# Engine orders by list scheduling, folding by column blocks and held weight loads in a linear-attention and gated-FFN kernel

## The chip, the cores and the metric

One core of a Trainium2 chip. The metric is device time in microseconds (us) of the whole program, on real inputs, with results compared with the reference. A bank is one of eight pieces, of 512 columns each, of the memory that matmuls write (PSUM); the programs here let results in the same bank take turns. The granted clock is the share of TensorE's full clock that the profile shows as let through. Engines: PE (TensorE matmul), PEld (its weight loads), DVE (VectorE), ACT (ScalarE), POOL (GpSimd), SP (which issues DMAs).

## The reference

```python
xn = layernorm(x)                                    # x: 2048 tokens x 512
out = x + A(xn) + B(xn)

# A: linear attention, 32 heads of 16
q, k, v = split(xn @ wqkv)
pq, pk  = q @ w_phi, k @ w_phi                       # per head
phi(p)  = concat(softmax(p), softmax(-p))            # for pq and pk
kv = phi_k^T v ; z = sum(phi_k) ; o = (phi_q kv) / (phi_q z + 1e-6)
A  = o @ wo
# B: gated FFN, 512 -> 1376 -> 512
B  = (gelu(xn @ w_gate) * (xn @ w_up)) @ w_down
```

Both kernels multiply `w_phi` into the Q and K weights first ("folding"), so that one projection gives `pq` or `pk`. The softmax denominators of K are row sums of exponentials; they are put on the values (value scaling), so that the sum over tokens (value accumulation, `kv_acc`) is a plain matmul chain.

## The kernel before

Tokens come in 16 tiles of 128. A tile is normalised on DVE, transposed (the first four on PE, the other twelve by DMA), projected to Q, K and V on PE, and exponentiated on ACT. POOL makes the row sums of the K exponentials in four steps, and the reciprocal standard deviation of the normalisation (`rstd`); DVE scales the values; PE accumulates them. The FFN follows in four chunks of 512 tokens, with 11 column blocks each; values that are not done by then, attention and output go beside it. The program is written in one sequence, and each engine runs its part in exactly that sequence. Waits are derived from buffers read and written. A unit, in the code, is one K or Q projection with what is written beside it; K and Q take two banks in turn. The parts that matter (cut):

```python
def op(self, ename, fn, reads=(), writes=(), extra=()):
    E = self.engs[ename]
    waits = self._resolve(E, self._deps_of(reads, writes, extra))
    ...
    E.ops.append((waits, fn, (E.sem, 1)))        # order on an engine = order of writing
...
proj_k(3, 1)
for t in range(8, 12):
    ln_stats(t)                                  # DVE, ahead of values 1 and 2
ln_rstd(8, 4)
v_recip(1); v_scale(1, 2)
v_recip(2); v_scale(2, 3)
...
units = []                                       # K and Q alternate
for s in range(3):
    for m in range(4):
        units.append(("k", 4 + 4 * s + m)); units.append(("q", s, m))
for m in range(4):
    units.append(("q", 3, m))
for u, un in enumerate(units):
    b = u % 2
    if u in (1, 2, 3, 4):      ln_norm(7 + u); xt_dma(7 + u)       # tiles 8 to 11
    ...
    if u in (10, 11, 12, 13):  ln_norm(2 + u); xt_dma(2 + u)       # tiles 12 to 15
    ... # proj_k or proj_q of the unit
    if u < 3:                  kv_acc(u)
    if u % 4 == 3:             proj_v(nv, 4); v_recip(nv); v_scale(nv, 4); nv += 1
    if u % 4 == 1 and u > 4:   kv_acc(nv - 1)
    if u % 3 == 2 and nbig < 5:
        big_loads(nbig); nbig += 1               # gate, up, wo, down: issued on POOL
```

wq is transposed by DMA; wk by PE, with two copies of 128x1024. Each fold makes a row block of the folded weights and needs all transposed columns.

The softmax here doesn't subtract the row's maximum and nothing guards it: scores larger than these inputs give would overflow.

Of the kernel before, what the change touches and what calls it, by code (L numbers as in the profile page):

```python
# [6 lines left out]
ALU = mybir.AluOpType  # L7
ACTF = mybir.ActivationFunctionType

P = 128  # L10
# [14 lines left out]
class _Handle:  # L25
    __slots__ = ("key", "val", "sem", "clock")

    def __init__(self, key, val, sem, clock):
        self.key = key
        self.val = val  # L30
        self.sem = sem
        self.clock = clock


class Buf:

    def __init__(self, name, aliases=()):
        self.name = name
        self.last_write = None
        self.readers = []  # L40
        self.aliases = list(aliases)


class _Eng:
    def __init__(self, name, sem):
        self.name = name
        self.sem = sem
        self.ops = []
        self.count = 0
        self.known = {}  # L50


class _DmaSlot:
    def __init__(self, sid, sem):
        self.sid = sid
        self.sem = sem
        self.count = 0
        self.last = None


class Sched:
    def __init__(self, eng_sems, dma_sems):
        self.engs = {n: _Eng(n, s) for n, s in eng_sems.items()}
        self.pools = {}
        k = 0
        for qn, sems in dma_sems.items():
            slots = []
            for s in sems:
                slots.append(_DmaSlot(k, s))
                k += 1  # L70
            self.pools[qn] = [slots, 0]

    def _resolve(self, E, deps):
        need = {}
        for h in deps:
            if h is None:
                continue
            if E.known.get(h.key, 0) >= h.val:
                continue
            cur = need.get(h.key)  # L80
            if cur is None or cur.val < h.val:
                need[h.key] = h
        waits = []
        for key in sorted(need.keys(), key=lambda x: str(x)):
            h = need[key]
            if E.known.get(key, 0) >= h.val:
                continue
            waits.append((h.sem, h.val))
            if E.known.get(key, 0) < h.val:
                E.known[key] = h.val  # L90
            for k2, v2 in h.clock.items():
                if E.known.get(k2, 0) < v2:
                    E.known[k2] = v2
        return waits

    @staticmethod
    def _deps_of(reads, writes, extra):
        deps = list(extra)
        for b in reads:
            deps.append(b.last_write)  # L100
            for a in b.aliases:
                deps.append(a.last_write)
        for b in writes:
            deps.append(b.last_write)
            deps.extend(b.readers)
            for a in b.aliases:
                deps.append(a.last_write)
                deps.extend(a.readers)
        return deps

    @staticmethod
    def _update(h, reads, writes):
        for b in reads:
            b.readers.append(h)
        for b in writes:
            b.last_write = h
            b.readers = []

    def op(self, ename, fn, reads=(), writes=(), extra=()):
        E = self.engs[ename]  # L120
        waits = self._resolve(E, self._deps_of(reads, writes, extra))
        E.count += 1
        idx = E.count
        clock = dict(E.known)
        clock[E.name] = idx
        h = _Handle(E.name, idx, E.sem, clock)
        E.ops.append((waits, fn, (E.sem, 1)))
        self._update(h, reads, writes)
        return h

    def dma(self, qname, fn, reads=(), writes=(), extra=()):
        E = self.engs[qname]
        slots, nxt = self.pools[qname]
        slot = slots[nxt % len(slots)]
        self.pools[qname][1] = nxt + 1
        deps = self._deps_of(reads, writes, extra)
        if slot.last is not None:
            deps.append(slot.last)
        waits = self._resolve(E, deps)
        slot.count += 1  # L140
        val = 16 * slot.count
        key = ("d", slot.sid)
        clock = dict(E.known)
        clock[key] = val
        h = _Handle(key, val, slot.sem, clock)
        E.ops.append((waits, fn, (slot.sem, 16)))
        slot.last = h
        self._update(h, reads, writes)
        return h

    def all_slots(self):
        res = []
        for qn, (slots, _) in self.pools.items():
            res.extend(slots)
        return res


def _replay(eng, E):
    for waits, fn, inc in E.ops:
        for sem, val in waits:  # L160
            eng.wait_ge(sem, val)
        ins = fn(eng)
        if inc is not None:
            ins.then_inc(inc[0], inc[1])


def bass_parallel_sum__linear_kernel_hedgehog__glu_gated_geglu__prompt_kernel(
# [14 lines left out]
    with ExitStack() as es, nc.allow_low_precision("bf16 softmax factors"):  # L182
# [34 lines left out]
        wk_nat = hT[:, 1, 0:4, :]  # L217
        wkT = hT[:, 1, 4:8, :]
        wqT = hT[:, 0, 0:4, :]

# [4 lines left out]
        NVS = 3  # L225
# [28 lines left out]
        def bank16(b):  # L254
# [6 lines left out]
             "act": [sem(f"dq_act{i}") for i in range(4)],  # L261
             "pool": [sem(f"dq_pool{i}") for i in range(6)]},
        )
        op = S.op
        dma = S.dma

        def bufs(name, n):
            return [Buf(f"{name}{i}") for i in range(n)]

# [6 lines left out]
        B_hT = bufs("hT", 2)  # L276
        B_wknat = Buf("wknat", aliases=[B_hT[1]])
        B_wkT = [Buf(f"wkT{i}", aliases=[B_hT[1]]) for i in range(2)]
        B_wqT = Buf("wqT", aliases=[B_hT[0]])
        B_hT[1].aliases = [B_wknat] + B_wkT  # L280
        B_hT[0].aliases = [B_wqT]
# [3 lines left out]
        B_Ek = bufs("Ek", NT)  # L285
        B_st = bufs("st", 3)
        B_S = bufs("S", NT)
        B_vs = bufs("vs", NVS)
        B_Eq = bufs("Eq", NST * 8)
        B_kvr = Buf("kvr")  # L290
        B_kvrm = Buf("kvrm")
        B_r, B_t, B_den, B_rden, B_cf, B_o = (bufs(n, NB) for n in ("r", "t", "den", "rden", "cf", "o"))
# [4 lines left out]
        B_ob = bufs("ob", 4)  # L297


        def load_x(t, extra=()):  # L300
            dma("sp", lambda e, t=t: e.dma_start(x_all[:, t, :], x2[t * P:(t + 1) * P, :]), writes=[B_x[t]], extra=extra)

        dma("act", lambda e: e.dma_start(
            wphi[:], A_w_phi.rearrange("(j hl) d f -> (hl d) j f", j=4)), writes=[B_wphi])
        load_x(0)
        dma("act", lambda e: e.dma_start(
            wk_nat, A_wqkv[:, 512:1024].rearrange("(i p) c -> p i c", p=P)), writes=[B_wknat])
        load_x(1)
        dma("act", lambda e: e.dma_start(
            wv_sb[:], A_wqkv[:, 1024:1536].rearrange("(i p) c -> p i c", p=P)), writes=[B_wv])  # L310
        load_x(2)
        load_x(3)
        load_x(4, extra=[B_wknat.last_write])
        for t in range(5, 8):
            load_x(t)
        dma("sp", lambda e: e.dma_start_transpose(wqT, A_wqkv[:, 0:512]), writes=[B_wqT])
        for t in range(8, NT):
            load_x(t)


        op("dve", lambda e: e.memset(warm[:], 0.0), writes=[B_warm])
        op("pool", lambda e: e.memset(ones_f[:], 1.0), writes=[B_ones])
        op("pool", lambda e: e.memset(neghalf[:], -0.5), writes=[B_nh])
        op("pool", lambda e: e.affine_select(
            idt_f[:], ones_f[:], pattern=[[-1, 128]], compare_op=ALU.is_equal,
            fill=0.0, base=0, channel_multiplier=1), reads=[B_ones], writes=[B_idf])
        op("pool", lambda e: e.tensor_copy(ident[:], idt_f[:]), reads=[B_idf], writes=[B_ident])
        op("pool", lambda e: e.affine_select(
            m8t[:], ones_f[:, 0:8], pattern=[[-16, 8]], compare_op=ALU.is_ge,
            fill=0.0, base=0, channel_multiplier=1), reads=[B_ones], writes=[B_m8t])  # L330
        op("pool", lambda e: e.affine_select(
            mask8[:], m8t[:], pattern=[[16, 8]], compare_op=ALU.is_ge,
            fill=0.0, base=15, channel_multiplier=-1), reads=[B_m8t], writes=[B_mask8])

        def ln_stats(t):
            op("dve", lambda e, t=t: e.bn_stats(stats[:, t, :], x_all[:, t, :]),  # L336
               reads=[B_x[t]], writes=[B_stats[t]])
            op("dve", lambda e, t=t: e.bn_aggr(mv[:, t, :], stats[:, t:t + 1, :]),  # L338
               reads=[B_stats[t]], writes=[B_mv[t]])

        def ln_rstd(t, n):
            op("dve", lambda e, t=t, n=n: e.tensor_scalar(
                vpe[:, t:t + n], mv[:, t:t + n, 1], 1e-5, None, op0=ALU.add),
               reads=B_mv[t:t + n], writes=B_vpe[t:t + n])
            op("pool", lambda e, t=t, n=n: e.tensor_tensor(  # L345
                rstd[:, t:t + n], vpe[:, t:t + n], neghalf[:, 0:n], op=ALU.pow),
               reads=B_vpe[t:t + n] + [B_nh], writes=B_rstd[t:t + n])
# [69 lines left out]
        def vs_view(t):  # L417
            return vs[:, t % NVS, :, :].rearrange("p s (h c) -> p s h c", c=VW)

# [400 lines left out]
```

## Time and profile before

| | before |
|---|---|
| time, median | 217.42 us (217.30 to 218.41, 4 runs) |
| span of the profiled run (time 218.12 us) | 216.6 us |
| first FFN matmul | 66.5 us |
| last matmul starts | 213.1 us |

The page's first and fourth parts (busy us and share of the span; then the chain that ended last, by engine):

```profile
...
PE 199.5 (92%) x1094; PEld 98.3 (45%) x1115; DVE 134.0 (62%) x302; ACT 75.8 (35%) x133; POOL 83.9 (39%) x114
...
PE 78%; DVE 13%; DMA 3%; POOL 2%; issue 2%; ACT 1%; ACTq 0%; DVEq 0%
...
```

PE is the longest resource and nearly the whole of the chain. Busy time hides a part of the truth, because a matmul's record is 379 ns while matmuls follow each other every 216 ns (16 of them take 3.45 us in the chain). So the stages have to be looked at one by one. These are windows of the span: each row has the window, then busy us and instructions of PE, PEld, DVE, ACT and POOL, the granted TensorE clock, the DMA share and GB/s:

```profile
...
5.60:15.00 9.40, 6.93 (x64) 4.26 (x64) 7.69 (x18) 4.39 (x7) 2.11 (x3) 1.00 0.97 251
15.00:25.00 10.00, 6.74 (x46) 3.23 (x45) 8.60 (x18) 8.37 (x16) 8.27 (x12) 1.00 0.40 97
25.00:35.00 10.00, 8.04 (x46) 4.51 (x48) 9.06 (x14) 3.93 (x8) 9.22 (x16) 0.83 0.20 39
35.00:45.00 10.00, 8.85 (x46) 3.82 (x44) 6.78 (x11) 8.42 (x17) 9.40 (x13) 1.00 0.90 297
45.00:55.00 10.00, 8.01 (x40) 3.77 (x42) 5.85 (x8) 4.38 (x9) 9.25 (x15) 0.83 0.82 213
55.00:66.50 11.50, 11.35 (x65) 5.42 (x64) 3.39 (x4) 9.94 (x20) 10.55 (x18) 1.00 0.09 31
66.50:213.60 147.10, 145.22 (x785) 71.81 (x799) 89.38 (x225) 35.08 (x58) 32.92 (x31) 1.00 0.12 29
...
```

From 66.5 us on PE is full. Before that it is not, and in two windows its clock is granted only to 0.83, while POOL is busy throughout from 25 us. Where PE stands still is seen in its timeline (start, duration, engine, line, instruction, shapes, count, and in brackets the idle time before and what ended it):

```profile
...
21.92 0.63 PE L444 MATMUL ps_all<-vs,Ek 128*128 128x136 bf16 x8
22.61 0.81 PE L399 MATMUL ps_all<-xnT,wq 128*128 128x512 bf16 x3
26.96 0.76 PE L444 MATMUL ps_all<-vs,Ek 128*128 128x136 bf16 x8 [3.54 <-DVE vs L428]
27.51 1.91 PE L375 MATMUL ps_all<-wk,xnT 128*128 128x512 bf16 x4
...
```

The second accumulation (26.96) waited 3.54 us for the value scaling on DVE, which stood behind the statistics of four later tiles. The four K matmuls after it took 1.91 us: 0.43 us apart instead of 0.216. The second stall in the chain of waits, in order of time (start, us, what):

```profile
...
39.27 1.18 POOL st L388
...
42.08 1.00 POOL rstd L345
...
44.27 0.88 DVE xn_sb L351
...
45.65 1.24 DVE vs L428
...
46.94 0.65 PE ps_all L444 x8
...
```

A row sum held POOL until 42.08, the `rstd` of tiles 12 to 15 stood behind it, their normalisations behind that, the value scaling behind those, and PE started again at 46.94.

To compare kernels I count what PE lost in a stage: the time from one weight load to the next (every matmul has one, and none is missing from the records) less the pitch of its matmul at full clock, read from the same traces (0.216 us for 512 columns, 0.059 for a value accumulation, 0.063 for attention, 0.056 for a transpose or fold). Idle time and slow clock both count; the last stage is counted up to the start of the last matmul. Before, the loss is 16.5 us up to 68 us and 2.6 us after it.

### The profile page before, as it was taken

The page shows a single profiled execution, that of the slowest core. Times are in us where ns is not written, and L with a number is a line of the kernel's source. Part 1 is how long each engine was busy: PE and PEld are TensorE (multiplying, and loading weights), DVE is VectorE, ACT ScalarE, POOL GpSimd, SP SyncE. Part 2 cuts the span into 40 slices and gives each one's busy share as a digit, 9 for nine tenths or more (in the row PEclk, how much of TensorE's full clock was granted, in tenths as well). Part 3 has the DMA queues.
Part 4 walks back from the last instruction along what each step waited for, and adds up shares of the span by engine and source line. Part 5 has one row for each costly group of instructions (what it writes and reads, how often), then busy time and mean ns, then how long its engine had stood idle before and what let it go on. Part 6 is the DMA issues. An engine that isn't in the chain of part 4 may idle for free.

```text
span 216.6 us, 3003 instructions
## 1 busy us (share of the span) xinstructions
PE 199.5 (92%) x1094; PEld 98.3 (45%) x1115; DVE 134.0 (62%) x302; ACT 75.8 (35%) x133; POOL 83.9 (39%) x114
## 2 busy tenths in 40 slices
PE   7776399949999999999999999999999999998994
PEld 2433154424444554554444455544455444543441
DVE  4698988593335877799459575494744777622121
ACT  2449537836886222232312313232232231422000
POOL 3219999999994000022424124323323222440200
PEclk9999969997999999999999999999999999999999
DMA  6892216969300000002020112101140111110101
GB/s 155 250 267 61 49 24 109 390 203 229 123 0 3 0 0 0 3 0 48 24 52 25 24 48 50 26 24 24 48 51 0 50 48 27 48 24 24 47 29 48
DMA packets 24590, 14.40 MB, mean 66 GB/s; under 512 B 18464, under 2 KB 23584, under 8 KB 24576
## 3 DMA queue, kind: packets, MB, share of 16 engines
q1 hardware_dynamic: 21920, 8.39, 17.0%
q0 software_dynamic: 1072, 4.75, 6.6%
q10 hardware_dynamic: 1584, 1.07, 1.8%
q8 instruction: 9, 0.15, 0.3%
q14 instruction: 5, 0.04, 0.1%
HBM read 7.91 MB, written 2.10 MB: 46 GB/s over the span
## 4 chain that ended last, share of the span: by engine, by line
PE 78%; DVE 13%; DMA 3%; POOL 2%; issue 2%; ACT 1%; ACTq 0%; DVEq 0%
PE ps_all L472 32%; PE ps_all L567 18%; PE ps_all L562 6%; PE ps_all L399 5%; PE ps_all L412 5%; PE ps_all L375 4%; PE ps_all L493 4%; PE ps_all L444 4%; DVE stats L336 3%; DMA hT<-in_A_wqkv_dram 3%; DVE xn_sb L351 2%; DVE vs L428 2%; POOL rstd L345 1%; DVE otmp L539 1%; DVE mv L338 1%
## 5 line engine op out<-in xcount | busy, mean ns | idle before, releaser
L485 DVE TENSOR_TENSOR hT<-gs,ps_all 128x512 bf16<-128x512 bf16 (+1 forms) x44 | 30.1, 683 | 31.9 <-PE ps_all L493 23.2
L482 ACT ACTIVATE gs<-ps_all 128x512 bf16<-128x512 f32 (+1 forms) x44 | 26.2, 597 | 57.0 <-PE ps_all L472 47.0
L472 PE MATMUL ps_all<-xnT,wg_sb 128*128 128x512 bf16 (+1 forms) x175 | 45.1, 379 | 0.1
L472 PE MATMUL ps_all<-xnT,wu_sb 128*128 128x512 bf16 (+1 forms) x170 | 44.5, 379 | 0.3
L567 PE MATMUL ps_all<-wd_sb,hT 128*128 128x512 bf16 (+1 forms) x171 | 40.4, 379 | 0.3
L551 POOL TENSOR_TENSOR o_sb<-otmp 128x512 bf16<-128x512 bf16 x16 | 18.4, 1152 | 54.6 <-DVE otmp L539 54.6
L582 POOL TENSOR_TENSOR ob<-y_sb,x_all 128x512 bf16<-128x512 f32 x12 | 13.8, 1153 | 47.3 <-ACT y_sb L580 47.3
L428 DVE TENSOR_TENSOR vs<-ps_all,vs 128x1024 bf16<-128x1024 f32 x16 | 19.6, 1227 | 14.2 <-PE ps_all L412 14.1
L472 PEld LDWEIGHTS ps_all<-xnT,wu_sb 128*128 128x128 bf16 (+1 forms) x176 | 17.6, 100 | 20.4
L567 PEld LDWEIGHTS ps_all<-wd_sb,hT 128*128 128x128 bf16 (+1 forms) x176 | 17.2, 98 | 20.8
L472 PEld LDWEIGHTS ps_all<-xnT,wg_sb 128*128 128x128 bf16 (+1 forms) x176 | 17.0, 100 | 16.6
L380 ACT ACTIVATE Ek<-ps_all 128x512 bf16<-128x512 f32 x32 | 17.2, 597 | 14.5 <-PE ps_all L375 14.4
L580 ACT ACTIVATE y_sb<-ps_all 128x512 f32<-128x512 f32 x12 | 7.2, 597 | 41.7 <-PE ps_all L567 41.7
L539 DVE TENSOR_TENSOR otmp<-ps_all,cf 128x384 bf16<-128x384 f32 (+1 forms) x48 | 21.5, 504 | 0.0
L388 POOL TENSOR_TENSOR st<-Ek 128x512 f32<-128x512 bf16 x16 | 18.6, 1160 | 0.1
L406 ACT ACTIVATE EqT<-ps_all 128x512 bf16<-128x512 f32 x32 | 17.2, 605 | 2.5 <-PE ps_all L399 2.3
L375 PE MATMUL ps_all<-wk,xnT 128*128 128x512 bf16 x61 | 17.0, 405 | 0.6 <-ACT Ek L380 0.3
L399 PE MATMUL ps_all<-xnT,wq 128*128 128x512 bf16 x63 | 17.3, 402 | 0.1
L412 PE MATMUL ps_all<-wv_sb,xnT 128*128 128x512 bf16 x61 | 16.2, 387 | 0.7 <-DMA wv_sb<-in_A_wqkv_dram 0.6
L444 PE MATMUL ps_all<-vs,Ek 128*128 128x136 bf16 x128 | 10.8, 230 | 6.6 <-DVE vs L428 6.6
L562 PE MATMUL ps_all<-wo_sb,oT 128*128 128x512 bf16 x62 | 16.0, 379 | 0.8 <-ACT y_sb L580 0.8
L351 DVE TENSOR_SCALAR xn_sb<-x_all,mv,rstd 128x512 bf16<-128x512 bf16 x16 | 12.1, 797 | 4.8 <-POOL rstd L345 4.8
(56 smaller groups left out, 171.9 us busy)
## 6 DMA issues: line engine op xcount, KB each, us to landing
x_all<-in_A_x_dram SPq DMA_DIRECT2D x16, 128.0 KB, 3.1
out_dram<-ob SPq DMA_DIRECT2D x16, 128.0 KB, 1.7
wg_sb<-in_B_w_gate_dram POOLq DMA_DIRECT2D x1, 1376.0 KB, 7.3
wu_sb<-in_B_w_up_dram POOLq DMA_DIRECT2D x1, 1376.0 KB, 7.3
wd_sb<-in_B_w_down_dram POOLq DMA_DIRECT2D x1, 1280.0 KB, 7.6
hT<-in_A_wqkv_dram ACTq DMA_DIRECT2D x1, 512.0 KB, 5.8
wv_sb<-in_A_wqkv_dram ACTq DMA_DIRECT2D x1, 512.0 KB, 7.1
wo_sb<-in_A_wo_dram POOLq DMA_DIRECT2D x1, 512.0 KB, 4.8
```

Of the source, the lines that this page charges most:

```text
L375: h = op("pe", lambda e, i=i, t=t, b=b: e.matmul(bank(b), xnT[:, i, t * P:(t + 1) * P], wk2[:, i, :], start=(i == 0), stop=(i == 3)), read ...
L388: op("pool", lambda e: e.tensor_tensor(v1, ev[:, :, 0:8], ev[:, :, 8:16], op=ALU.add), reads=[B_Ek[t]], writes=[B_st[0]])
L399: h = op("pe", lambda e, i=i, p=p, s=s, b=b: e.matmul(bank(b), wq2[:, i, p * 128:(p + 1) * 128], xnT[:, i, s * 512:(s + 1) * 512], start=( ...
L412: h = op("pe", lambda e, i=i, t=t, b=b: e.matmul(bank(b), xnT[:, i, t * P:(t + 1) * P], wv_sb[:, i, :], start=(i == 0), stop=(i == 3)), re ...
L428: h = op("dve", lambda e, v=v, b=b: e.tensor_tensor(v[:, :, :, 0:DH], bank(b).rearrange("p (h d) -> p h d", d=DH).unsqueeze(1).to_broadcas ...
L444: h = op("pe", lambda e, t=t, i=i, sig=sig, p=p, b=b, st=st: e.matmul(bank(b)[:, (i % 3) * GV:(i % 3 + 1) * GV], Ek[:, t, sig, p * 128:(p ...
L472: h = op("pe", lambda e, i=i, s=s, jf=jf, w=w, wt=wt, b=b: e.matmul(bank(b)[0:w, :], wt[:, i, jf * 128:jf * 128 + w], xnT[:, i, s * 512:(s ...
L482: op("act", lambda e, w=w, k=k, J=J: e.activation(gs[0:w, k, :], bank(J % 2)[0:w, :], ACTF.Gelu_apprx_tanh), reads=[BK[J % 2]], writes=[B_ ...
L485: h = op("dve", lambda e, w=w, k=k, J=J, s=s, jf=jf: e.tensor_tensor(hT[0:w, s % 2, jf, :], gs[0:w, k, :], bank(2 + J % 2)[0:w, :], op=ALU ...
L539: op("dve", lambda e, q=q, n=n: e.tensor_tensor(otmp[:, k, q * 384:q * 384 + n * 128].rearrange("p (s h d) -> p s h d", s=n, d=DH), bank(4 ...
L562: h = op("pe", lambda e, j=j, t=t, b=b: e.matmul(bank(b), oT[:, t % NOT, j, :], wo_sb[:, j, :], start=(j == 0), stop=False), reads=[B_oT[t ...
L567: h = op("pe", lambda e, jf=jf, w=w, s=s, tl=tl, b=b: e.matmul(bank(b), hT[0:w, s % 2, jf, tl * 128:(tl + 1) * 128], wd_sb[0:w, jf, :], st ...
```

## The change

Its intent: let a list scheduler with planned costs choose the order of each engine instead of the order of writing; fold in column blocks, so that folds and copies of one block overlap those of the next; transpose wq on PE as wk; move four of the sixteen row sums to DVE; give the values five buffers instead of three; and keep the FFN weight loads (4.75 MB) back: the gate weights until the transpose of tile 11 is done, the others until that of tile 15, the last. The core of the diff (cut; scheduling costs and mechanical rewriting left out):

```diff
+    def schedule(self):
+        ...
+        while len(order) < len(self.ops):
+            ...                                  # engine that can start first, at time t
+            h = min((x for x in cand[n] if x.ready <= t + 1e-9), key=lambda x: x.prio)
+            ...
+            free[n] = t + h.cost
-        wk_nat = hT[:, 1, 0:4, :]
-        wkT = hT[:, 1, 4:8, :]
+        wkT = hT[:, 1, 0:4, :]
+        wk_nat = hT[:, 1, 4:8, :]
         wqT = hT[:, 0, 0:4, :]
+        wq_nat = hT[:, 0, 4:8, :]
-        NVS = 3
+        NVS = 5
-        dma("sp", lambda e: e.dma_start_transpose(wqT, A_wqkv[:, 0:512]), writes=[B_wqT])
+        load_w(wq_nat, 0, B_wqn, 8.0)
...
-            op("dve", lambda e, t=t, n=n: e.tensor_scalar(
+            op("pool", lambda e: e.tensor_scalar(
                 vpe[:, t:t + n], mv[:, t:t + n, 1], 1e-5, None, op0=ALU.add),
...
+        SDVE = (9, 11, 13, 15)
+            if t in SDVE:
+                op("dve", lambda e: e.tensor_reduce(Ssum[:, t, :], ev, axis=mybir.AxisListType.X, op=ALU.add), ...
+                return
...
+        def fold(wT, BwT, w2, B_w2, j, b):
+            op("pe", [lambda e, i=i: e.matmul(
+                bank(b)[:, i * 128:(i + 1) * 128], wT[:, j, i * 128:(i + 1) * 128], bd[:, j, :],
+                start=True, stop=True) for i in range(4)], reads=[BwT[j], B_bd], ...
...
+        def big_loads():
+            x = [d_xt[15]]                       # the last DMA transpose
+            dma("pool", ... wg_sb ..., extra=[d_xt[11]], prio=-500)
+            dma("pool", ... wu_sb ..., extra=x, prio=-500)
+            ...                                  # wo, down: extra=x
+        for s in range(NST):
+            if s < NST - 1:
+                ln_group(4 * s + 4)              # ahead of the rest by 60 places
+            if s == 2:
+                big_loads()
+            for m in range(4):
+                proj_k(4 * s + m, kq())          # kq(): banks 0, 1, 2 in turn
+                if m % 2 == 1 or nv < 4:
+                    val()
+            for m in range(4):
+                proj_q(s, m, kq())
+                ...
```

PE's real work is nearly the same: 16 transposes of wq are new. The diff also changes things: three banks in turn for K and Q instead of two, more banks for the values, finer tracking of buffers (by column block, half or bank), and copies that the scheduler may give to ACT or DVE.

## The prediction

> **What bounds it now.** PE: 199.5 us busy of a 216.6 us span; the chain of waits is 78% PE, 13% DVE. The two halves differ. Busy time by stretch: from the first FFN matmul (66.5 us) to the last matmul (213.6) PE is busy 145.2 of 147.1 us; from 5.6 to 66.5 it is busy 49.9 of 60.9, and that flatters it, because a matmul's record (379 ns) overlaps the next.
>
> Useful work by issue pitch (in the chain eight FFN matmuls take 1.73 us, eight value accumulations 0.47, eight attention matmuls 0.50): before the FFN 64 K, 64 Q and 40 V matmuls (36.3 us), nine accumulations (4.2), 64 transposes and folds (3.5): 44 us of work in the 59.4 us from 7.1 to 66.5, so 15 us lost. After it 592 FFN and output matmuls (127.7), 24 V (5.2), seven accumulations (3.3), 16 attentions (8.0): 144 us in 147. The tail is 3 us.
>
> Where the 15 us go (timeline, waits): K starts only at 14.5, after whole-matrix fold steps; PE stands 3.5 us near 23.5 to 27 and 3.0 near 44 to 47, both released by the value scaling on DVE, which stands in fixed order behind later tiles' statistics and behind normalisations that wait for rstd on POOL. After each stall K and Q run at half rate for about 3 us (granted clock 0.74 to 0.92 there), as the Trainium skill's "TensorE: Matmul & The Clock Gate" (The HAM clock gate) describes: an idle window halves the clock. That is 3 to 4 of the 15 us.
>
> **What the change does.**
> - Removed: the DMA transpose of wq (4.9 us to landing), four row-sum chains from POOL (2.6 us each; POOL is busy 48.8 of the 60.9 us), the order stalls, most half-clock time.
> - Added: 16 PE transposes of wq (1.1 us), about four net PSUM copies of 0.6 us, four DVE row sums (estimate 1.2 us each, from the 1.23 us value scaling of 1024 elements).
> - Moved: folding by column block overlaps copies and folds on two engines; I estimate the first K at 11 to 12 us. FFN weights (7.3 us per 1.4 MB) wait for the transposes and should still land by about 48.
> - Unchanged: PE's matmul work. ACT's 64 exponentials at a 0.54 us pitch are 35 us, so ACT cannot finish before about 50; DVE's normalisation (16 x 1.6), values (10 x 1.7) and sums are about 50 us too. Values that slip land beside the first FFN chunk, where DVE has slack.
>
> **Sum.** Ideal: start 7.1 + matmuls 184.8 + transposes and folds 5 + tail 3 = 200 us of span. I expect 4 to 6 us of remaining loss (fold latency at 7 to 12; ACT, DVE and PE nearly equal before the FFN; planned costs too low: normalisation is planned at 0.42 us and took 0.80). Span about 205, time 1 us more: 206 us, 8 in 10 between 201 and 212. Chances: faster 0.90, same 0.07, slower 0.03.
>
> **What would show it.** First FFN matmul at 50 to 57 instead of 66.5; first K exponential near 12 to 13 instead of 15.6; no PE gap over 2 us after 12; granted clock 0.95 or more after 10; FFN stretch 145 to 151 us, values included; ACT busy over 85% between 13 and 50.
>
> **What would make it wrong.** The order is frozen from modelled times: a POOL load waiting for a late transpose would block row sums behind it; DVE slowed beside POOL could starve values and PE; weights landing late could delay the first FFN chunk.

## The result, and the profile after

| | before | after |
|---|---|---|
| time, median | 217.42 us | 205.95 us (205.80 to 207.07, 4 runs) |
| span of the profiled run | 216.6 us | 204.1 us |
| first FFN matmul | 66.5 us | 55.0 us |
| PE's loss until 68 us / later | 16.5 / 2.6 us | 4.9 / 0.5 us |

The times of the kernel before scatter on every chip (from 215.7 to 218.6 us in the batches below; medians 216.1 to 217.5), so the ratios of one batch count. Its one profile is of a slow execution (218.12 us), and the profile after of a fast one (205.89 us): the 12.5 us between the spans are more than the 11.5 us between the medians. The ratio is 0.9474, with a 95% interval of 0.9431 to 0.9518. Ratios here are the mean time of one kernel's runs over that of the other's of the same rounds, so not quite the ratio of the medians. Executions over 1.5% slower than the fastest of the same kernel are left out of the means. The changed kernel is 5.3% faster.

The page's first and fourth parts after:

```profile
...
PE 194.8 (95%) x1109; PEld 98.2 (48%) x1131; DVE 134.9 (66%) x303; ACT 75.8 (37%) x136; POOL 76.1 (37%) x106
...
PE 82%; DVE 7%; DMA 3%; POOL 2%; ACT 2%; issue 1%; SPq 1%
...
```

The windows, with the last one from the first FFN matmul on:

```profile
...
5.60:15.00 9.40, 7.52 (x77) 4.86 (x76) 7.54 (x19) 4.82 (x9) 2.88 (x7) 1.00 0.71 232
15.00:25.00 10.00, 9.25 (x55) 4.38 (x56) 8.42 (x21) 9.47 (x20) 6.38 (x10) 1.00 0.42 105
25.00:35.00 10.00, 9.09 (x51) 4.27 (x51) 9.86 (x16) 8.89 (x19) 9.27 (x15) 1.00 0.32 61
35.00:45.00 10.00, 9.89 (x73) 5.60 (x73) 9.26 (x13) 7.39 (x15) 9.19 (x15) 1.00 0.65 188
45.00:55.00 10.00, 9.50 (x55) 4.67 (x55) 7.24 (x10) 7.73 (x17) 8.75 (x14) 1.00 0.78 265
55.00:201.20 146.20, 145.23 (x797) 73.00 (x811) 89.71 (x222) 36.22 (x61) 37.01 (x36) 1.00 0.14 34
...
```

The clock is 1.00 in all of them, and PE's busy time is above 9 us in every full 10-us window from 15. The FFN stage is as long as before, 146.2 us against 147.1. The gain is therefore before the FFN: 11.5 of the 12.5 us of span. PE's timeline at the places that answer to the stalls shown of before:

```profile
...
17.57 3.40 PE L396 MATMUL ps_all<-wk,xnT 128*128 128x512 bf16 x15 [0.32 <-ACT wq L587]
...
29.48 1.04 PE L432 MATMUL ps_all<-wv_sb,xnT 128*128 128x512 bf16 x4 [0.64 <-DVE vs L442]
...
34.19 2.07 PE L458 MATMUL ps_all<-vs,Ek 128*128 128x136 bf16 x32 [0.22 <-DVE vs L442]
36.30 1.67 PE L396 MATMUL ps_all<-wk,xnT 128*128 128x512 bf16 x7
...
```

The longest wait in brackets after 15 us is 0.64 us, and the first four accumulations come together at 34.19, when all four values are ready. Nothing runs at half clock. But K starts late: its first matmul is at 17.57 (14.5 before). The K projections take the same three banks after wq's transposes and folds, so they come behind these (14.21 to 17.25 on PE) and behind ACT's last copy of the folded wq (0.32 us of waiting).

The loads, in the timeline of POOL:

```profile
...
33.02 1.00 POOL L645 DMA_DIRECT2D wg_sb<-in_B_w_gate_dram  x1
...
45.77 0.82 POOL L648 DMA_DIRECT2D wu_sb<-in_B_w_up_dram  x1 [0.79 <-DMA xnT<-xn_sb]
46.58 0.75 POOL L651 DMA_DIRECT2D wo_sb<-in_A_wo_dram  x1
47.32 0.96 POOL L654 DMA_DIRECT2D wd_sb<-in_B_w_down_dram  x1
...
```

The up weights waited 0.79 us for the last transpose, landed in 7.2 us at 53.0, and the first up matmul came at 57.2. There is no slack of many microseconds on either side.

The sum nearly closes: the loss fell by 11.7 us before 68 us and by 2.1 us after it, the added transposes cost 0.9 us (16 at 0.056), which makes 12.9 us against 12.5 us of span.

### The profile page after: what moved, and what is told of

Its sections match the earlier page's. It is cut to its first block, busy times and chain, and to the rows that moved or that the text cites. A ratio compares the mean times of both kernels' runs of the same rounds, so it can differ in the third digit from the quotient of the medians.

```text
span 204.1 us, 2998 instructions
## 1 busy us (share of the span) xinstructions
PE 194.8 (95%) x1109; PEld 98.2 (48%) x1131; DVE 134.9 (66%) x303; ACT 75.8 (37%) x136; POOL 76.1 (37%) x106
## 3 DMA queue, kind: packets, MB, share of 16 engines
q0 software_dynamic: 1072, 4.75, 6.8%
## 4 chain that ended last, share of the span: by engine, by line
PE 82%; DVE 7%; DMA 3%; POOL 2%; ACT 2%; issue 1%; SPq 1%
PE ps_all L484 36%; PE ps_all L558 19%; PE ps_all L554 7%; PE ps_all L432 6%; PE ps_all L506 4%; PE ps_all L458 4%; PE ps_all L396 4%; PE ps_all L421 3%; DMA x_all<-in_A_x_dram 3%; DVE vs L442 2%; DVE xn_sb L375 2%; POOL st L411 1%; DVE stats L360 1%; ACT hT L579 1%; DVE vs L439 1%
## 5 line engine op out<-in xcount | busy, mean ns | idle before, releaser
L490 DVE TENSOR_TENSOR hT<-gs,ps_all 128x512 bf16<-128x512 bf16 (+1 forms) x44 | 29.1, 682 | 26.1 <-PE ps_all L484 26.1
L484 PE MATMUL ps_all<-xnT,wu_sb 128*128 128x512 bf16 (+1 forms) x174 | 45.1, 379 | 0.3
L546 POOL TENSOR_TENSOR o_sb<-otmp 128x512 bf16<-128x512 bf16 x16 | 18.4, 1152 | 69.3 <-DVE otmp L540 69.3
L484 PE MATMUL ps_all<-xnT,wg_sb 128*128 128x512 bf16 (+1 forms) x168 | 43.8, 379 | 0.3
L427 ACT ACTIVATE EqT<-ps_all 128x512 bf16<-128x512 f32 x32 | 16.5, 654 | 3.3 <-PE ps_all L421 3.3
L400 ACT ACTIVATE Ek<-ps_all 128x512 bf16<-128x512 f32 x32 | 16.3, 620 | 3.3 <-PE ps_all L396 3.1
L523 DVE RECIPROCAL r_sb<-ps_all 128x48 f32<-128x48 f32 (+1 forms) x32 | 9.3, 327 | 10.0 <-PE ps_all L506 9.9
L411 POOL TENSOR_TENSOR st<-Ek 128x512 f32<-128x512 bf16 x12 | 13.9, 1161 | 2.7 <-ACT Ek L400 2.7
L421 PE MATMUL ps_all<-xnT,wq 128*128 128x512 bf16 x62 | 14.8, 379 | 0.1
L396 PE MATMUL ps_all<-wk,xnT 128*128 128x512 bf16 x61 | 14.3, 379 | 0.4 <-ACT wq L587 0.3
L360 DVE BATCH_NORM_STATS2 stats<-x_all 128x6 f32<-128x512 bf16 x16 | 10.8, 673 | 3.0 <-DMA x_all<-in_A_x_dram 3.0
```

The costliest lines, as they stand in the source:

```text
L396: op("pe", [lambda e, i=i: e.matmul(bank(b), xnT[:, i, t * P:(t + 1) * P], wk2[:, i, :], start=(i == 0), stop=(i == 3)) for i in range(4)] ...
L421: op("pe", [lambda e, i=i: e.matmul(bank(b), wq2[:, i, p * 128:(p + 1) * 128], xnT[:, i, s * 512:(s + 1) * 512], start=(i == 0), stop=(i = ...
L427: exps.append(op("act", lambda e, g=g, sig=sig: e.activation(EqT[:, g, s * 512:(s + 1) * 512], bank(b), ACTF.Exp, scale=(1.0, -1.0)[sig]), ...
L484: op("pe", [lambda e, i=i, wt=wt, b=b: e.matmul(bank(b)[0:w, :], wt[:, i, jf * 128:jf * 128 + w], xnT[:, i, s * 512:(s + 1) * 512], start= ...
L490: op("dve", lambda e: e.tensor_tensor(hT[0:w, s % 2, jf, :], gs[0:w, k, :], bank(ub)[0:w, :], op=ALU.mult), reads=[B_gs[k], BK[ub]], write ...
L546: op("pool", lambda e: e.tensor_tensor(o_sb[:, k, :], otmp[:, k, 0:512], otmp[:, k, 512:1024], op=ALU.add), reads=B_ot[k], writes=[B_o[k]] ...
```

## The experiments

The theory that I began with (A): the two DVE-order stalls and the half clock after each are the gain, some 10 us, and any order that avoids them would do. The rivals: POOL's row sums or the late K are the real bound (B); the relief of POOL (C); column folding (D); the quieter DMA.

### e1: mend the two stalls by hand in the kernel before

```diff
-        for t in range(8, 12): ln_stats(t)
-        ln_rstd(8, 4)
+        ln_stats(8); ln_stats(9)
         v_recip(1); v_scale(1, 2)
+        ln_stats(10); ln_stats(11); ln_rstd(8, 4)
         v_recip(2); v_scale(2, 3)
-            if u < 3: kv_acc(u)
+            if u in (2, 4, 6): kv_acc(u // 2 - 1)
-            if u in (10, 11, 12, 13): ln_norm(2 + u); xt_dma(2 + u)
+            if u in (12, 13, 14, 15): ln_norm(u); xt_dma(u)
```

> The kernel before, with only the order of three things mended by hand: values 1 and 2 scaled between the statistics of tiles 8 to 11 instead of after them, the first three value accumulations put later on PE (units 2, 4, 6 instead of 0, 1, 2), the normalisations of tiles 12 to 15 two units later, behind value 5. Nothing else of the change. Theory A (the gain is the two DVE-order stalls of 3.9 and 3.4 us and the half clock after each, about 3 us together): both PE stalls shrink below 1 us, no stretch under a granted clock of 0.95 after 15 us, the first FFN matmul at about 57 and the time 207 to 211 us. Rival B (the row sums on POOL, or the late start of K, are the bound, and the stalls only move elsewhere): the time stays above 214 us and new PE waits of several us appear before 66 us.

Measured: 218.57 us (216.82 to 220.02), ratio 1.0075 (1.0003 to 1.0147). The waits of PE from 5 to 70 us (who waited for whom: us in total, times, longest):

```profile
...
PE ps_all L444 <- DVE vs L428: 4.7, 1, 4.7
PE ps_all L375 <- DMA xnT<-xn_sb: 3.1, 1, 3.1
...
```

Both old stalls went and two new ones came, of 4.7 and 3.1 us. PE, earlier by the first repair, reached the accumulation of value 3, whose scaling stood behind three normalisations; and tile 12, normalised later and transposed beside a weight load, landed late (6.2 us after its issue, where the median of the run is 2.5). Theory A in its simple form falls. The stalls move: rival B was right about the movement, though not yet about the cause.

### e2: keep PE warm in the stalls of the kernel before

```diff
+        def filler(b):                           # 12 matmuls of no use into bank b
+            for m in range(12):
+                op("pe", lambda e, b=b: e.matmul(bank(b), warm[:, 0:128], warm[:], start=True, stop=True), ...)
             if u < 3:
+                if u == 1: filler(4)
                 kv_acc(u)
             if u % 4 == 1 and u > 4:
+                if u == 13: filler((u + 1) % 2)
                 kv_acc(nv - 1)
```

> The kernel before, with twelve matmuls of no use put into a free bank in each of the two stalls (before the accumulations of values 1 and 5), so PE stands still for about 1 us instead of 3.9 and 3.4. The waits stay. If the half clock after the stalls comes from the idle time (theory A), K and Q matmuls after them keep 0.216 us each, granted clock stays near 1.0 and the time falls by 2 to 4 us, to 213.5 to 215.5. If the half rate has another cause (waits for semaphores, or slow loads), or is hidden behind ACT and POOL, the time stays at 216.5 to 218.

Measured: 215.95 us (215.88 to 216.57), ratio 0.9968 (0.9926 to 1.001): between the two expectations, and in timed runs not clear of zero. The profiled span is 214.4 us instead of 216.6, with the first FFN matmul 2.2 us earlier; but PE's loss before 15 us, which the edit does not reach, is 0.6 us smaller too, so the stages from 15 us on give 1.6 us (the added matmuls counted as lost). Windows of this run:

```profile
...
25.00:30.00 5.00, 3.83 (x30) 1.95 (x28) 4.30 (x6) 1.41 (x3) 4.69 (x7) 1.00 0.00 0
...
45.00:50.00 5.00, 4.58 (x28) 2.21 (x27) 3.87 (x6) 2.06 (x4) 4.70 (x8) 1.00 0.90 179
...
```

Before, the granted clock of these two windows was 0.74 and 0.78 (0.92 and 0.87 in the 5 us after each), which is about 3.4 us of lost clock, within the 3 to 4 that I predicted. So the idle time causes the half clock, as the Trainium skill's page "TensorE: Matmul & The Clock Gate" (The HAM clock gate) says of idle windows of about 3.4 us, and this trace agrees: from one weight load to the next the two stalls lasted 4.1 and 3.6 us before, and at most 1.5 us here. But what comes of it is 1.6 us by the profiles and less in the timed runs, since PE runs into the next wait sooner.

### e3: release the FFN loads earlier in the changed kernel

```diff
-            x = [d_xt[15]]
+            x = [d_xt[11]]
-                wg_sb ... extra=[d_xt[11]], prio=-500)
+                wg_sb ... extra=[d_xt[7]], prio=-500)
```

> The changed kernel, unaltered, on the same chip as the next three, to compare them with: 205.5 to 206.5 us, span 204, first FFN matmul at 55.

> The changed kernel, with the FFN loads released earlier: the gate weights after the transpose of tile 7 instead of 11, the other four after tile 11 instead of 15, so that 3.3 MB run beside the transposes of tiles 12 to 15. If holding the loads is worth much (rival: the gain is the quieter DMA), transposes land in 5 to 7 us instead of 2.5 and the time rises by over 2 us. If it is worth little (theory A: the order of DVE and PE is the gain), the time is within 1.5 us of the unaltered kernel; the plan of the list itself moves a little too.

Measured on one chip: the unaltered kernel 205.98 us (ratio 0.9515, 0.9469 to 0.9561), with earlier loads 211.39 us (ratio 0.9777, 0.9723 to 0.983). That is 5.4 us, nearly half of the gain. Theory A's expectation was wrong again. (An edit of the changed kernel makes the scheduler plan anew: a comparison of the traces finds 64 of 1131 weight loads on PE and 19 of 106 instructions on POOL at another place in e3, and 30 to 86 weight loads in e4 to e8. So each of these runs tests an edit together with its new plan.) The chain of waits of this run tells how (start, us, what):

```profile
...
30.17 3.86 DMA xnT<-xn_sb
...
34.32 0.78 POOL wu_sb L648
35.10 0.75 POOL wo_sb L651
...
36.19 1.05 POOL rstd L369
...
37.27 3.94 DVE xn_sb L375 x4
...
41.71 1.24 DVE vs L442
...
43.00 3.56 PE ps_all L458 x32
...
```

A transpose that landed at 34.0, slowed beside the gate weights (the eight transposes of tiles 8 to 15 take 3.9 to 10.0 us here, against 2.4 to 3.5 in the changed kernel), held the up load; the load stands in POOL's order, so POOL stood too; two loads were issued; only then came the `rstd` of tiles 12 to 15; DVE's normalisations waited 3.9 us for it; the value scaling stood behind them; and PE stood for 3.9 us and then ran at half clock. It is the failure that the prediction had named ("a POOL load waiting for a late transpose would block row sums behind it"), brought about by a release 8 us (gate) and 11.5 us (up) earlier.

### e4 and e5: all row sums on POOL; folding by rows

```diff
-        SDVE = (9, 11, 13, 15)
+        SDVE = ()
```

> The changed kernel, with all sixteen row sums on POOL (four go back from DVE: 4 x 2.6 us more on POOL, 4 x 1.2 us less on DVE). Rival C (relief of POOL is a main part of the gain): POOL is busy to about 70 instead of 60, values wait for it, the time rises by 3 us or more. Theory A: values slip further beside the first FFN chunk, where DVE and PE have other work, and the time rises by 0 to 1.5 us.

Measured: 207.38 us (206.74 to 207.54), ratio 0.9558 (0.9518 to 0.9599), 1.4 us above the unaltered kernel of the same chip.

```diff
-                bank(b)[:, i * 128:(i + 1) * 128], wT[:, j, i * 128:(i + 1) * 128], bd[:, j, :],
-                start=True, stop=True) for i in range(4)], reads=[BwT[j], B_bd], ...
-            dst, src = w2[:, :, j * 128:(j + 1) * 128], bank(b).rearrange("p (i c) -> p i c", i=4)
+                bank(b)[:, i * 128:(i + 1) * 128], wT[:, i, j * 128:(j + 1) * 128], bd[:, i, :],
+                start=True, stop=True) for i in range(4)], reads=BwT + [B_bd], ...
+            dst, src = w2[:, j, :], bank(b)
```

> The changed kernel, with folding by row blocks as before: each fold needs all four transposed column blocks. Theory A: K starts only after the fold of wq (the same three banks), so the folds of wk are not what the first K waits for; time within 1 us of the unaltered kernel. Rival D (folding in column blocks is a main part): the first K exponential 1 us or more later and the time up by 1 to 2 us.

Measured: 207.33 us (206.91 to 209.08), ratio 0.9582 (0.9533 to 0.963), 1.35 us above the unaltered kernel. The intervals of both overlap that of the unaltered kernel, so either is at most a small part, by the medians a bit over 1 us. On the same chip five of the six runs of the unaltered kernel lie at 206.04 us or less, and all runs of e4 and e5 at 206.74 or more. Counted as above, e4 loses 1.0 us more than the changed kernel after 68 us, where one value accumulation waits 1.2 us, and e5 1.2 us more up to 68 us. Rivals C and D do not carry the gain.

### e6, e7, e8: the start of the changed kernel

e6 writes the transposes and folds of wq after the second K projection:

```diff
-        for j in range(4): wtrans(wq_nat, B_wqn, wqT, B_wqT, j, kq())
-        for j in range(4): fold(wqT, B_wqT, wq2, B_wq2, j, kq())
...
                 proj_k(4 * s + m, kq())
+                if s == 0 and m == 1:
+                    fold_q()                     # the two lines above
```

> The changed kernel, with the transposes and folds of wq written after the second K projection instead of before the first, so K need not wait for wq (the prediction's step of an early first K, which the trace contradicts: 18.4 instead of 12 to 13). If an early first K were worth its time, the first K exponential comes near 14 and the time falls by 1 to 3 us. If ACT and PE only need it for balance later (theory A2), the time stays within 1 us.

Measured: 207.68 us (207.44 to 209.12), ratio 0.9569 (0.9533 to 0.9604). In ACT's timeline the first K exponential comes 3 us earlier than the changed kernel's 18.42:

```profile
...
15.43 2.06 ACT L400 ACTIVATE Ek<-ps_all 128x512 bf16<-128x512 f32 x4 [1.73 <-PE ps_all L396]
...
```

The time did not fall: PE lost 2.6 us between 15 and 25 us (0.85 in the changed kernel), since the copies of wq now wait between exponentials (and 1.6 us between 35 and 45, where the changed kernel loses none). So a first K made early by putting wq off gains nothing; one made early by faster folds, as I had predicted, was not run. (e6 to e8 ran on a chip without the unaltered kernel; on two other chips its median was 205.95 and 205.98 us.)

e7 transposes wq by DMA again:

```diff
-        load_w(wq_nat, 0, B_wqn, 8.0)
         d_x4 = load_x(4, 4, 4.5, [d_wk])
+        dma("sp", lambda e: e.dma_start_transpose(wqT, A_wqkv[:, 0:512]), writes=B_wqT, cost=2.0, lat=3.5, prio=-900)
-        for j in range(4): wtrans(wq_nat, B_wqn, wqT, B_wqT, j, kq())
```

> The changed kernel, with wq transposed by DMA again, as before the change: 16 PE transposes and four copies less (0.9 us of PE, 2.4 us of ACT and DVE), one DMA transpose (4.9 us to landing) more. If the move of wq to PE is part of the gain, the time rises by 1 us or more, because the transpose delays the x tiles behind it on its queue. If not, the time falls by 0 to 1.5 us.

Measured: 205.59 us (204.87 to 207.37), ratio 0.948 (0.9438 to 0.9522): the same as the changed kernel. The move of wq to PE is no part of the gain.

e8 loads wq only when wk has landed:

```diff
-        load_w(wq_nat, 0, B_wqn, 8.0)
+        dma("sp", lambda e: e.dma_start(wq_nat, ...), writes=B_wqn, lat=5.0, prio=-900, extra=[d_wk])
```

> The changed kernel, with the load of wq issued only when wk has landed, so that x tiles 2 and 3 share the DMA with 0.5 MB less; PE stood still 0.8 and 1.1 us for them at 6.6 and 8.0 us. If the late x tiles set the pace of the first 15 us, tile 3 lands 1 us earlier, PE's loss there halves and the time falls by 0.5 to 1.5 us; if the rest of the chain (wq's folds before the first K) sets it, the time is within 0.5 us or rises.

Measured: 206.53 us (206.28 to 208.43), ratio 0.9534 (0.9488 to 0.958): no gain. No version of these beats the changed kernel clearly.

### e9, e10, e11: order and held loads in the kernel before

After e1 and e3 I held another theory (A2): order and held loads belong together, and the other parts matter little. e9 holds the loads alone:

```diff
-            if u % 3 == 2 and nbig < 5:
+            if u in (10, 18, 19, 20, 21):
                 big_loads(nbig); nbig += 1
```

> The kernel before, with only the FFN loads moved later: the gate weights at unit 10 instead of 2, the other four at units 18 to 21 instead of 5, 8, 11 and 14, so that they follow the transposes of tiles 8 to 11 and of 12 to 15. If holding the loads is by itself worth what the early loads cost the changed kernel (rival B1: about 5 us), the time falls to 211 to 214 and the second PE stall (3.4 us near 44) goes. If the hold only matters in a schedule that is otherwise tight (theory A2: order and hold belong together), the first stall of 3.9 us stays, the second shrinks by at most 2 us, and the time is 214.5 to 217.5.

Measured: 215.76 us (215.52 to 215.91), ratio 0.9937 (0.9869 to 1.0004). As A2 said: the first stall stayed (3.5 us), the second shrank to 1.25 us, and the first FFN matmul came at 62.4 instead of 66.5. A new stall came: the up load stood behind POOL's row sums until 58.3 and PE waited 1.7 us for it.

e10 writes the whole order before the FFN anew by hand, after the changed kernel's:

```diff
-        NVS = 3
+        NVS = 5
-        proj_k(3, 1)
         for t in range(8, 12): ln_stats(t)
         ln_rstd(8, 4)
+        proj_k(3, 1)
+        for t in range(8, 12): ln_norm(t); xt_dma(t)
         v_recip(1) ...
-        ... units: K and Q alternate
+        ... units: four Q, then four K
+            if u in (6, 7, 8, 9): ln_stats(6 + u)            # rstd of 12 to 15 at u == 9
+            if u in (13, 14, 15, 16): ln_norm(u - 1); xt_dma(u - 1)
+            if u in (12, 13, 14, 15): kv_acc(u - 12)
+            if u in (17, 21, 25, 27): kv_acc({17: 4, 21: 5, 25: 6, 27: 7}[u])
+            if u in (3, 11, 15, 19, 23, 27): ... value nv, in banks 4, 2, 3 in turn
+            if u in (14, 20, 21, 22, 23): big_loads(nbig); nbig += 1
```

> The kernel before, with its order written anew by hand after the changed kernel's (all four Q of a chunk, then four K; statistics and normalisations of tiles 8 to 11 ahead of values 1 to 3; the first four value accumulations together at unit 12; five value buffers; three banks for values; FFN loads held as in the previous run). Folding by rows, the DMA transpose of wq and all row sums on POOL stay as before. Theory A2 (order and hold are most of the gain): first FFN matmul at 57 to 60, no PE stall over 1.5 us, no low clock, 207 to 211 us. Rival D2 (the other parts are needed: folding, wq by PE, sums moved from POOL): stalls move once more and the time stays above 213.

Measured: 216.72 us (216.54 to 217.32), ratio 0.999 (0.9931 to 1.0048). By its time rival D2 was right: it is unchanged. But not the profile: PE's timeline at the start of the FFN:

```profile
...
56.65 1.03 PE L472 MATMUL ps_all<-xnT,wg_sb 128*128 128x512 bf16 x4
62.31 1.03 PE L472 MATMUL ps_all<-xnT,wu_sb 128*128 128x512 bf16 x2 [4.64 <-DMA wu_sb<-in_B_w_up_dram]
...
```

The first FFN matmul is at 56.65 instead of 66.5: the order, with five value buffers, more banks for the values and held loads, brought it forward by 9.9 of the change's 11.5 us. Then PE waited 4.64 us for the up weights, and ran at half clock after it. POOL worked on row sums some 14 us behind PE, and the load stood in its order; it was issued at 55.6.

e11 moves only the loads in that order:

```diff
-            if u in (14, 20, 21, 22, 23):
+            if u in (5, 12, 16, 17, 18):
```

> The hand-written order of the previous-but-one batch in the kernel before, with one difference: the FFN loads stand earlier in the queue of POOL (units 5, 12, 16, 17, 18 instead of 14, 20, 21, 22, 23). There POOL ran some 14 us behind PE, so a load held behind its row sums was issued at 55.6 and PE waited 4.6 us for the up weights at 57.6, then ran at half clock. Now gate should be issued near 34 and up near 44.5, and land near 52. Theory A2 (order, with the loads placed to suit it, is most of the gain): first FFN matmul at 56 to 58, no wait for weights, time 207.5 to 210.5 us, that is 7 to 10 of the 11.5 us without column folding, wq by PE or row sums on DVE. Rival D2 (those parts are needed): above 213.

Measured: 214.33 us (214.10 to 214.85), ratio 0.9882 (0.9839 to 0.9925): a small gain. Theory A2 missed its time and its first FFN matmul (61.1 instead of 56 to 58); by the time D2 was right again (above 213), but its reason, that the other parts are needed, is not what the trace shows. PE's timeline:

```profile
...
46.21 1.03 PE L375 MATMUL ps_all<-wk,xnT 128*128 128x512 bf16 x4
50.44 1.89 PE L375 MATMUL ps_all<-wk,xnT 128*128 128x512 bf16 x4 [3.20 <-DMA xnT<-xn_sb]
```

And the chain just before it:

```profile
...
40.72 1.00 POOL rstd L345
...
44.29 6.10 DMA xnT<-xn_sb
...
```

Now the up weights were issued at 44.4, as planned, landed in time, and ran beside the transposes of tiles 12 to 15: the first of them, issued at 43.1, still landed in 2.5 us, but the second, shown above, took 6.1, and PE waited 3.2 us for it. The `rstd` of these tiles was at 40.7, behind eight row sums on POOL; in the changed kernel it was at 35.9, behind five.

PE's loss by stage, in us, counted as told above:

| stage (us) | before | e1 | e9 | e10 | e11 | after | e3 |
|---|---|---|---|---|---|---|---|
| 5.6 to 15 | 3.4 | 3.0 | 2.8 | 2.6 | 2.6 | 2.2 | 1.9 |
| 15 to 25 | 6.1 | 2.8 | 6.1 | 3.1 | 3.1 | 0.9 | 0.9 |
| 25 to 35 | 1.8 | 5.9 | 1.6 | 1.7 | 1.7 | 1.4 | 1.4 |
| 35 to 45 | 3.3 | 1.5 | 1.7 | 0.1 | 0.1 | -0.2 | 5.3 |
| 45 to 55 | 1.6 | 4.8 | 0.1 | 0.3 | 4.7 | 0.6 | 0.4 |
| 55 to 68 | 0.3 | 0.3 | 2.0 | 6.9 | 0.1 | 0.0 | 0.0 |
| after 68 | 2.6 | 2.7 | 2.6 | 2.7 | 2.7 | 0.5 | 0.5 |

(The negative entry comes from the pitch, which is rounded. Up to 15 us e1 and e9 to e11 run the code of the kernel before, so the 0.4 to 0.8 us that they lose less there is the scatter of executions.) The load of the up weights takes 6.7 to 8.1 us, and has to fall between the last transposes and the first FFN matmul. Too late, as in e9 and e10, PE waits for the weights; too early, as in e3 and e11, transposes are late and all that hangs on them. The changed kernel finds room by having `rstd` and transposes of the last tiles done sooner. The three terms in which e11 is still behind (15 to 25: 2.2 us; 45 to 55: 4.1; after 68: 2.2) make 8.5 us, as much as the 8.4 us between the medians.

Not run: the order of e11 with a load that fits the gap, and the list order inside the FFN alone. So it stays open whether the old code could get down to about 210 by hand (214.3 less the 4.1 us, an estimate from the table), and what in the list order brings the 2.1 us after 68 us. The traces say where these are: 1.1 us is one standstill near the end, where PE waits 0.8 us for ACT to empty the bank in which it wants to start the next output (before, e1, e9, e10 and e11 have it, the changed kernel not); weight loads of the attention waited 2.3 us for DVE before, and 0.7 us after. The three K and Q banks and the finer tracking of buffers were not tried in the old code either.

## Why the prediction was right or wrong

- The time: 206 predicted, 205.95 measured. The sum that gave it held: 200 us of useful work, start and tail, and 4 to 6 us of remaining loss. The loss was 5.4 us. That the 4 to 6 us held is a good estimate and not a derivation, and the agreement to 0.05 us is luck: the span was 204.1 us where I had said about 205, and the time 1.8 us more than the span where I had said 1. The first FFN matmul fell in the range (55.0 in 50 to 57), as did the FFN stage (146.2 in 145 to 151) and PE's longest wait (under 2 us). The clock was 1.00 in the profiled run, though another profile of the same kernel had 0.70 from 10 to 15 us and was 2 us longer.
- Wrong: "I estimate the first K at 11 to 12 us", and the first K exponential "near 12 to 13". It was at 18.4, later than before. The step overlooked that K takes the banks after wq's folds. PE's loss there is small all the same (2.2 us from 5.6 to 15, 0.9 from 15 to 25), because PE fills the time with V projections and with wq's transposes and folds; e6 shows that one way to an earlier K gains nothing. ACT was busy 83% between 13 and 50 (30.8 of 37 us), under the 85% named.
- Too simple: "Removed: the order stalls", as if each had its own price. e1 removed both in the old kernel and gained nothing: a value scaling behind three normalisations (4.7 us) and a late transpose (3.1 us) became the next stalls. The total did not suffer from it, because the sum was made from PE's work and one figure for the loss, not from the stalls one by one.
- Half clock: 3 to 4 us predicted. The lost clock in the profile before is about 3.4 us; taking it away alone (e2) gave 1.6 us by the profiles, and nothing clear in the timed runs.
- Under-rated: the held loads. The prediction treated them as a risk only ("should still land by about 48"). The up weights landed at 53.0, in time by 4 us, and releasing them 8 to 11.5 us earlier costs 5.4 us (e3). The Trainium skill's page "DMA: Bandwidth & Descriptors" (Issuing engines are not separate DMA queues) says that DMAs of all engines run on the same 16 DMA engines and interleave; e3 and e11 agree, with transposes issued by SP slowed from 2.4 to 7.4 us (e11) and 10.0 us (e3) at the most beside loads issued by POOL.
- Row sums on DVE, column folding and wq by PE, which the prediction listed side by side with the order, are worth 1.4, 1.35 and 0 us by the medians, the first two not clear of zero.
- Planned costs: the plan has 0.42 us for a normalisation. In DVE's timeline four of them took 1.38 us while POOL was idle (from 17.53) and 2.82 us beside its row sums (from 24.87), which is what the Trainium skill's page "SBUF — State Buffer" (Who interferes with whom) describes for DVE and GpSimd sharing a port. What it cost PE was not measured.

## What to carry to other kernels

Where several engines and DMAs are all near full in one stage, price a change by the main engine's loss over the whole stage: removing one stall shows only the next. A load that is issued in an engine's own order is both a DMA and a place in that order; look at the gap that it must fit, between the last small transfer that it would slow and the first use, and at what stands behind it in the queue. When the order is frozen from planned costs, test its tight places by moving one release, as here, before touching arithmetic.

## What the Trainium skill lacked or had wrong

- "DMA: Bandwidth & Descriptors" says, in its rules, that a transpose next to ordinary DMAs needs nothing. That is about correctness, and all runs were correct; no figure for its time beside a load was found there. Here a DMA transpose of a 128x512 tile lands in 2.4 to 2.6 us with no load beside it, and in 3.9 to 10.0 us beside the FFN loads (e3, tiles 8 to 15).
- "TensorE: Matmul & The Clock Gate" puts the cost of the clock's ramp under 1% of a typical span, and calls it run-variable. The cost seen here is of that size, but it came as a second fall after the clock had been full. The second profile of the changed kernel (a0, 206.2 us of span against 204.1) has a granted clock of 0.95 from 5 to 10 us, and then this window:

```profile
...
10.00:15.00 5.00, 4.95 (x35) 3.34 (x35) 3.14 (x7) 2.30 (x5) 0.27 (x1) 0.70 0.38 125
...
```

The granted clock of 0.70 is 1.5 us of lost clock, 0.7% of the span; in the first profile it is 1.00 there. The longest wait of PE before it was 1.0 us, so the clock fell without a stall like those of the kernel before; why is open. The timed runs fall in two groups too (205.8 to 206.0, and 207.1 to 208.0 us). That is as large as several of the effects tested, so one profile does not settle a question of 1%.
